# A two-attention, two-convolution kernel: all six instruction orders rewritten, finer pool waits, whole-row statistics for three blocks

## The chip, the cores and the metric

One core of a Trainium2 chip runs the whole program. Its engines work in parallel, each through its own list of instructions in order: TensorE (PE, matmuls into PSUM), VectorE (DVE), ScalarE (ACT), GpSimd (POOL), and SyncE (SP), which here issues nearly all DMAs. The metric is device time in microseconds, and less is better. The profile is one execution, recorded instruction by instruction.

## The reference

The input `x` has 2048 rows of 512 columns (bf16). Four residual layers follow one another, with the same weights for both layers of a kind:

```python
x = x + _A_ref(_layernorm(x), A_wqkv, A_wo)          # attention
x = x + _B_ref(_layernorm(x), B_A_re, ..., B_Dskip)  # convolution
x = x + _A_ref(_layernorm(x), A_wqkv, A_wo)
x = x + _B_ref(_layernorm(x), B_A_re, ..., B_Dskip)
```

`_A_ref` projects to queries, keys and values with 32 heads of 16 columns. Each row attends to 8 rows: itself and those 2, 4, ... 14 rows earlier (earlier than the first row: masked). Softmax over the 8, weighted sum of values, projection by `wo`. `_B_ref` is a long convolution: per column a kernel of 2048 taps is made from 128 complex exponentials, `K[d, l] = Re sum_n C[d,n] exp(dt[d] A[d,n] l) dt[d] B[d,n]`; `K` and the layer's input are transformed by FFT, multiplied and transformed back; the input times `Dskip` is added.

## The kernel before

Row `16 p + a` of `x` lies in partition `p` (0 to 127), slot `a` (0 to 15). A *block* is four slots (512 rows), so there are four blocks.

The order of the work is written out by hand in six strings. A character or token is one step, and each string is walked from left to right; what a step issues goes to the end of the lists of the engines that it uses. So a string sets the order on every engine at once. Engines still run ahead of each other, held by semaphores alone.

**ORDERK** (`k_gen`): the convolution's taps and the front of the first attention. `s`, `i` square the complex exponentials (`s` on ACT, `i` on DVE), `b` copies powers into the tables `B_t` and `pow_t` on ACT, `c` copies a plane of `pow_t` by DMA, `C` and `M` are complex products on DVE, `G` builds Fourier constants on ACT. `T` and `U` build the power table `A_t` on DVE in four column chunks, even chunks in one pair of tiles (`T`), odd ones in another (`U`); `H` opens the next chunk with an ACT copy, and the first `H` opens the second pair of tiles in a pool of its own. `p` are the matmuls that make taps from tables, `x` their evictions into the kernel rows `kgs`, which 24 DMAs store at the end. For the attention: `a` row statistics on ACT (blocks 0 to 2), `3` on DVE (block 3), `l` and `W` norms, `y` and `z` normalised rows, `t`/`e` transposes and evictions, `k`/`K` and `q`/`Q` projections and evictions, `E` and `o` shifted copies of keys, `X` the first three products of queries and keys, `Z` their sums.

**CORE0, CORE1** (`LayerA.core`): the rest of each attention. `m` multiplies queries by keys (DVE, `prod`), `l` sums over head columns (PE), `x`, `e`, `r`, `n`, `T` are the softmax, `v`/`q` projections, `P` multiplies attention by values (DVE, `pav`), `S` or `V` sums it (PE, in half or whole columns), `O` projects by `wo`, adds the residual and takes statistics; `b`, `d` are norm steps, `t` statistics on DVE, `a` and `f` the normalised row on DVE or ACT. In CORE0 `A` to `H` copy eight parts of the convolution kernel, on the engines that `KROWS` lists (D = DVE, A = ACT).

**ORDER0, ORDERF, ORDER1** (`FftB.run`): the convolutions. The last letter of a token is the engine of its eviction (A = ACT, D = DVE, G = POOL and DVE in turn, B = ACT and DVE in turn). `K` and `U` transform kernel and input, `k` and `u` do the second transform step (`u` evicts on ACT into `ub`), `m` multiplies the two spectra on DVE. There are 16 of each, eight per half of the columns. `y` (64-row matmuls) and `Y` (128-row) are the first inverse step, again 16: those of a half need all eight `m` of that half. `z g b` is the last inverse step for half `g` and block `b`; `w g c b` and `v g c b` do it for a quarter of the columns, for eight or four slots. On DVE it adds the residual, on ACT extra matmuls with the identity add it. All these matmuls go through four rotating PSUM buffers. In the first convolution `k` takes a buffer from a list, `m` gives two back and issues a store to `kf_dram`, and loads on SP swap rows; the 16th `K` adds eight buffers. In the second one `m` reads spectra that SP loads from `kf_dram`.

ORDERF ends the first convolution and begins the second attention: `h g b` takes statistics over half rows (four instructions of 256 columns), `H b` over whole rows (four of 512), `a`, `p`, `n` make norms and normalised rows, `T`, `E`, `P`, `Q` transpose, evict and project. A whole-row step needs both halves of its block, a half step one.

A pool that takes over the room of a closed pool waits, as a rule, for everything that used the old one. With `reuse_waits="tile"` a new tile waits only for the tiles whose room it takes.

Of the kernel before, what the change touches and what calls it, by code (L numbers as in the profile page):

```python
# [11 lines left out]
ALU = mybir.AluOpType  # L12
# [34 lines left out]
sCiibsCbiisCiiMbMCGMiMsabiMcbiasMbbCCaGiMMTsibGGTGTicMbGsbiaTbcisbbTTTMGiiTbTiMaGsaGGTMiGacMabTl  # L47
MlMMMWMlaiMsiMayMwMiMybyaTMysteMMqatMaaMkeMadTkqMialKMMlQMkWMlaqMMcbqykTQHqUaUKqQaakUTyqUkyqUUpU
KUkyUapxUxtaUpatpeUaldHQqeUqkKUkl3TT33TQkkxpWl3KxTpTxyxTylTWTpqlkyyTqpHKkzkQzxKUtkUktezUqqeUKTkT
kQKztktkTeeKkUkUKTTkkKUUUkUxUUpxEUpkxpUkUUkpEKkKqxpkUxoxpEoKXqUokUkQUpKxpZxXxZXZ  # L50
"""
ORDER0 = """
KD KA KA KA KD KA KD KA KD KA KD kA kD kA kA kD UA KD UA UD kA UA kD UA KD UA
UD UA KD kA u UD m UA KA u UD u UD m KA u kA m m UA u u kD m m u
UA u UD kA m UA kD kA u m kA kD u kA yA m YD m u m u YA u u m u
yA m m u yA m m YA yA yD yD
# [3 lines left out]
yA yA z01D yA z00D yA yD h00 yA h01 YA v100A v110A v102A v013A h10 a0 p0 n0G z02A v111A v101A S v112A  # L60
h02 h11 T0 E00A a1 E01A z13D p1 n1G v003A P03 Q00 h12 a2 P01 T1 E10A p2 P00 E11D n2G h03 P11 P12
P13 T2 E20A h13 a3 E21D P02 p3 n3D P22 P21 P10 T3 E30D E31D P23 P20 x1
"""
ORDER1 = """
UA UD UA UD UA UA UD UA UD UA UD u UD u u UA m u m u m UA m u m u
UD m m UA u m u m u u yA YA u m m u yD m YA m u u m m u yA
YA m yA YD w000D yA yA yD yA z03D yA w010D yA yD yA z02D v103A v113D v112D v102D v110D v100A v111D v101A
# [3 lines left out]
vvmvvlvmvvmlvxlemvrmnlqmqvlTvqlxevqmlvmvmPvvP1rnllxS0qTmqOeVmrqP4qSl2OPPSOSOPSmPP5On3l8ml6SPCOOV  # L71
AlxSPP7eOSrObSPn9POSdOESOPSPbDadBPfaGOtFOaaawVfHSbatO
"""
CORE1 = """
0m1l2ml3mvvqqlmmlmvqqvvllxmemqvlrnvvlmxTqqlvvmqlmvPvvvvmvqlleqVPrmxqmnqSTOePlPmSOPllSPOSPrOSnOPS
mOSPOblxOSPPdeOSrffbVPdfwOnPfVOPSOSPafbOPSdafftOSafatO
# [4 lines left out]
KROWS = "ADDAADAA"  # L81
# [913 lines left out]
def k_gen(tc, nc, a_consts, ins, kd, la, x_v, lnst, zero, b_consts):  # L995
# [3 lines left out]
    with ExitStack() as ctx:  # L999
# [94 lines left out]

        def power(k):
            if 3 <= k <= 7:
                nc.scalar.copy(Pw[:, :, k - 3, 1::2, :].rearrange("p c r x -> p r c x"), planes(k))
            else:
                nc.scalar.copy(Bt[:, :, :, B_L.index(1 << k), :], cur[k][:].rearrange("p r (q g) -> p r q g", g=4))

        def power_neg(k):
            nc.scalar.mul(Pw[:, :, k - 3, 2, :], planes(k)[:, 1], -1.0)
# [51 lines left out]
        def norms():  # L1154
            D2 = D * D
            for b in range(4):
                cs = slice(4 * b, 4 * b + 4)
                rstd = la.fp.tile([P, 4], F32, name="ln_rstd")
                nb = la.fp.tile([P, 4], F32, name="ln_nb")
                ln[b] = rstd, nb  # L1160
                if b < 3:
                    mean, ms = lnst["s1"][:, cs], -1.0 / D
                    msq = la.fp.tile([P, 4], F32, name="ln_msq")
                    veps = la.fp.tile([P, 4], F32, name="ln_veps")
                    lvar[b] = veps[:]
                    yield lambda: nc.vector.scalar_tensor_tensor(msq[:], mean, -1.0 / D2, mean, ALU.mult, ALU.mult)
                    yield lambda: nc.vector.scalar_tensor_tensor(veps[:], lnst["s2"][:, cs], 1.0 / D, msq[:], ALU.mult, ALU.add)
                else:
                    ag = la.fp.tile([P, 4, 2], F32, name="ln_ag")
                    lvar[b] = ag[:, :, 1]  # L1170

                    def aggr():
                        for a in range(4):
                            nc.vector.bn_aggr(ag[:, a, :], lnst["bn"][:, 12 + a, 0, :])

                    yield aggr
                    mean, ms = ag[:, :, 0], -1.0
                yield lambda: nc.vector.scalar_tensor_tensor(nb[:], mean, ms, rstd[:], ALU.mult, ALU.mult)
# [17 lines left out]
        def turned(b, d):  # L1196
            nc.scalar.copy(la.xnT[:, 2 * d:2 * d + 2, b * 512:(b + 1) * 512], xps[b, d][:].rearrange("p t a q -> p t (a q)"))
# [9 lines left out]
        def projected(kind, b, ft):  # L1207
            dst = la.kT[:, ft, 14 + b * 4:18 + b * 4, :] if kind == "k" else la.qT[b][:, ft]
            nc.scalar.copy(dst.rearrange("p a q -> p (a q)"), pps[kind, b, ft][:])  # L1209
# [3 lines left out]
        def stage_two():  # L1213
            c_small.close()
            tab.append(ctx.enter_context(tc.tile_pool(name="kg_tab1", bufs=1)))
            late["kgp"] = ctx.enter_context(tc.tile_pool(name="kg_out", bufs=1))
# [53 lines left out]
        def produced(c, q8):  # L1270
# [3 lines left out]
            nc.scalar.copy(late["kgs"][:, :, q0:q0 + 8].rearrange("p m (h j) -> p m h j", h=2),  # L1274
# [42 lines left out]
        def chain(*fs):  # L1317
# [3 lines left out]
        fts = range(NDT)  # L1321
# [4 lines left out]
            a=calls(pass_stats, *((b, a, i) for b in range(3) for a in range(4) for i in range(2))), l=norms(),  # L1326
            W=calls(inv_std, *((b,) for b in range(4))), y=calls(apply, *((b, a, "act") for b in range(3) for a in range(4))),
            z=calls(apply, *((3, a, "dve") for a in range(4))),
# [9 lines left out]
        ops["3"] = calls(lambda a: row_stats(nc, lnst, xb[3][:, a, :], 12 + a, "dve"), *((a,) for a in range(4)))  # L1338
# [240 lines left out]
```

## Time and profile before

| | us |
|---|---|
| median of 3 runs | 402.94 (402.64 to 403.21) |
| profiled execution | 402.72 |
| its span, first to last instruction | 400.8 |
| DVE busy | 381.5 (95%) |
| ACT busy | 326.0 (81%) |
| PE busy (matmuls) | 320.0 (80%) |
| POOL busy | 66.1 (17%) |

The granted TensorE clock is 0.999. Busy time is the union of an engine's instructions, which overlap a little: the time from start to start is shorter than the duration of one. A line of the timeline gives the start, the time, engine, source line, operation, result and operands, the number of like instructions merged, and in brackets idle time of that engine just before, with the engine whose work ended it. The largest groups are the DVE products of the attentions (`pav` at L465, 72.6 us in 34, and `prod` at L340, 66.6 us in 29) and the evictions of the convolutions on ACT (`ub` at L865, 31.9 us in 32).

### The profile page before, as it was taken

What the parts mean: (1) busy time and instruction counts of PE and PEld (TensorE: products, weight loads), DVE (VectorE), ACT (ScalarE), POOL (GpSimd) and SP (SyncE); (2) the same over time, 40 slices, a digit from 0 to 9 for tenths busy, and PEclk for the clock granted to TensorE, in tenths of its full rate; (3) what the DMA queues carried; (4) which work ended last, traced back from release to release, by engine and by line L of the source; (5) the groups of instructions that cost most, each with busy time, mean ns of one, the idle gap of its engine ahead of it and who ended that gap; (6) DMA issues with size and microseconds to landing.
All of it is one profiled execution on the core that took longest, in us unless ns stands there. A gap on an engine that the chain in (4) does not pass through costs nothing.

```text
span 400.8 us, 14761 instructions
## 1 busy us (share of the span) xinstructions
PE 320.0 (80%) x6479; PEld 227.6 (57%) x6527; DVE 381.5 (95%) x475; ACT 326.0 (81%) x565; POOL 66.1 (17%) x79
## 2 busy tenths in 40 slices
PE   3000178789999899889997889999999998998795
PEld 2000037557635567656887878643456766667785
DVE  6999999999999999999999999979999999989995
ACT  7999999786656499888999998864655788989983
POOL 9402500000299600030500002300000001000000
PEclk9999999999999999999999999999999999999999
DMA  7942820323014855285235677740063009504606
GB/s 220 395 132 31 87 65 12 83 54 94 12 39 110 216 180 152 79 296 225 101 115 206 223 270 215 263 136 2 2 169 94 3 20 404 162 2 108 213 11 205
DMA packets 62322, 54.17 MB, mean 135 GB/s; under 512 B 33869, under 2 KB 50738, under 8 KB 60978
## 3 DMA queue, kind: packets, MB, share of 16 engines
q1 hardware_dynamic: 62250, 53.22, 43.6%
q8 instruction: 51, 0.84, 0.9%
q14 instruction: 13, 0.11, 0.1%
q10 hardware_dynamic: 8, 0.00, 0.0%
HBM read 30.15 MB, written 13.24 MB: 108 GB/s over the span
## 4 chain that ended last, share of the span: by engine, by line
PE 29%; DVE 21%; issue 9%; ACT 7%; DMA 4%; SPq 1%; POOL 0%; DVEq 0%; ACTq 0%
DVE pav L465 5%; PE pq L396 5%; PE pq L501 4%; PE po L490 4%; DVE prod L340 3%; PE pq L221 3%; DVE t L849 3%; DVE t L852 3%; DVE ln_bn L148 2%; PE pb L799 2%; DMA v_ext<-v_ext 2%; PE L L352 2%; DVE a1s L788 1%; PE pb L806 1%; PE pb L883 1%
## 5 line engine op out<-in xcount | busy, mean ns | idle before, releaser
L465 DVE TENSOR_TENSOR pav<-attn,v_ext 128x4096 bf16<-128x4096 bf16 (+1 forms) x34 | 72.6, 2169 | 0.2
L340 DVE TENSOR_TENSOR prod<-qT,kT_ext 128x4096 bf16<-128x4096 bf16 x29 | 66.6, 2322 | 0.4 <-ACT qT L223 0.3
L1108 DVE TENSOR_TENSOR A_t<-A_t,pow_t 128x1024 bf16<-128x1024 bf16 (+4 forms) x46 | 37.9, 870 | 0.2
L1194 PE MATMUL pt<-ident,x_blk 128*128 128x128 bf16 x64 | 6.3, 241 | 39.6 <-ACT x_blk L193 39.6
L501 PE MATMUL pq<-wop,oT 128*128 128x512 bf16 x122 | 31.7, 379 | 3.4 <-issue 2.5
L490 PEld LDWEIGHTS <-pav 64*128 64x128 bf16 x1664 | 26.0, 95 | 13.4 <-DVE pav L465 6.0
L490 PE MATMUL po<-ident,pav 64*128 64x64 bf16 x1664 | 29.0, 190 | 4.2 <-DVE pav L465 2.3
L865 ACT CAST ub<-pb 128x1024 bf16<-128x1024 f32 x32 | 31.9, 1068 | 0.2
L398 ACT CAST v_ext<-pq 128x512 bf16<-128x512 f32 x32 | 18.8, 586 | 16.1 <-PE pq L396 16.1
L1204 PE MATMUL pp<-xnT,kT_ext 128*128 128x512 bf16 x88 | 25.3, 404 | 7.8 <-ACT qT L1209 2.8
L806 PE MATMUL pb<-a1s,w_sb 128*128 128x64 bf16 x768 | 27.3, 193 | 5.0 <-ACT a1s L788 3.1
L396 PE MATMUL pq<-wv,xnT 128*128 128x512 bf16 x120 | 29.9, 379 | 0.4
L806 PEld LDWEIGHTS <-w_sb 128*128 128x128 bf16 x768 | 24.8, 98 | 7.2 <-issue 4.8
L1194 PEld LDWEIGHTS <-x_blk 128*128 128x128 bf16 x64 | 4.7, 107 | 42.0 <-ACT x_blk L193 40.4
L788 DVE CAST a1s<-pb 128x1024 bf16<-128x1024 f32 x21 | 24.7, 1214 | 2.5 <-PE pb L799 2.2
L788 ACT CAST a1s<-pb 128x1024 bf16<-128x1024 f32 x27 | 26.4, 1043 | 0.8 <-PE pb L799 0.8
L1266 PEld LDWEIGHTS <-A_t 128*64 128x64 bf16 (+1 forms) x512 | 21.9, 103 | 4.7 <-DVE A_t L1108 0.6
L1266 PE MATMUL pk<-B_t,A_t 128*64 128x84 bf16 (+1 forms) x512 | 23.7, 201 | 1.0 <-ACT kgs L1274 0.5
L221 PE MATMUL pq<-xnT,kT_ext 128*128 128x512 bf16 x92 | 23.0, 379 | 0.2
L176 POOL TENSOR_TENSOR ln_rstd<-ln_rstd,ln_mh 128x4 f32<-128x4 f32 x2 | 4.0, 2016 | 107.4 <-DVE ln_rstd L175 107.4
L396 PEld LDWEIGHTS <-xnT 128*128 128x128 bf16 x128 | 11.7, 97 | 14.3 <-issue 1.7
L492 ACT CAST oT<-po 128x512 bf16<-128x512 f32 x26 | 14.9, 575 | 5.8 <-PE po L490 5.8
(261 smaller groups left out, 902.9 us busy)
## 6 DMA issues: line engine op xcount, KB each, us to landing
w_sb<-w_dram SPq DMA_DIRECT2D x8, 1024.0 KB, 6.8
w_dram<-xnT SPq DMA_DIRECT2D x1, 4096.0 KB
kf_ring<-kf_dram SPq DMA_DIRECT2D x13, 256.0 KB, 4.5
kf_ring<-kf_dram SPq DMA_DIRECT2D x26, 128.0 KB, 3.9
v_ext<-v_ext SPq DMA_DIRECT2D x4, 784.0 KB, 6.4
x_blk<-in_A_x_dram SPq DMA_DIRECT2D x4, 512.0 KB, 4.7
kT_ext<-in_A_wqkv_dram SPq DMA_DIRECT2D x4, 512.0 KB, 9.5
x_sb<-in_A_x_dram SPq DMA_DIRECT2D x4, 512.0 KB, 6.1
```

The lines of the kernel that those rows point to most:

```text
L221: nc.tensor.matmul(pq[:], lhsT=self.wqk[:, dt, ft * P:(ft + 1) * P], rhs=self.xnT[:, dt, q * 512:(q + 1) * 512], start=(dt == 0), stop=(dt ...
L340: nc.vector.tensor_tensor(pr, self.qT[q][:, ft].unsqueeze(1).to_broadcast([P, W, 4, P]), kap, ALU.mult)
L396: nc.tensor.matmul(pp[:], lhsT=xnT[:, dt, a * P:(a + 1) * P], rhs=wv[:, dt, :], start=(dt == 0), stop=(dt == NDT - 1))
L465: nc.vector.tensor_tensor(pv[:, i], attn[:, n % 4].unsqueeze(2).to_broadcast([P, W, DH // parts, H]), vap, ALU.mult)
L490: nc.tensor.matmul(po[:, h, 0, i * nt + ft, :], lhsT=pvf[rows, i, w, ft * P:(ft + 1) * P], rhs=ident[rows, rows], start=(w == 0 and ft + i ...
L501: nc.tensor.matmul(pw[:], lhsT=oT[:, ftp, :], rhs=self.wo[:, ftp, :], start=False, stop=(ftp == NDT - 1))
L788: (self.nc.scalar.copy if eng == "act" else self.nc.vector.tensor_copy)(dst, src)
L806: nc.tensor.matmul(p2[:, j, :], lhsT=self.w2[:, ec * EC + j, :], rhs=a1s[:, ec * EC + j, :], start=True, stop=True)
L865: nc.scalar.copy(ub[:], p2)
L1108: return lambda: nc.vector.tensor_tensor(*args)
L1204: nc.tensor.matmul(pps[kind, b, ft][:], lhsT=la.wqk[:, dt, c:c + P], rhs=la.xnT[:, dt, b * 512:(b + 1) * 512], start=(dt == 0), stop=(dt = ...
L1266: nc.tensor.matmul(o, lhsT=lhs, rhs=Bt[:, ri, c * CH + ql].rearrange("p b g -> p (b g)"), start=(not half and j % 4 == 0 and ri == 0), sto ...
```

## The change

All six strings are written anew. The choice of engine for many evictions, until now fixed in the code, is read from a table `ENGK`; as filled in, it differs from before in four places only: one `y` row goes from ACT to DVE, three of the four `z` rows of block 3 from DVE to ACT. `KROWS` gives DVE four parts rather than three. `STATD` names the block with DVE statistics, block 3 as before. The pools of the second power table and of the kernel rows get `reuse_waits="tile"`. In ORDERF three of the four blocks use `H` in place of two `h`. Inside the strings the engines shift too. On DVE are, before and after: in ORDER0 8 and 5 `K`, 6 and 7 `U`, 6 and 8 `k`; in ORDER0 and ORDERF together 4 and 4 `y` or `Y`, 3 and 2 `z`, 0 and 1 `v`; in ORDER1 4 and 5 `y` or `Y`, 4 and 1 `z` or `w`, 5 and 5 `v`; in CORE0 6 and 5 `a`; in CORE1 4 and 6 `a`.

```diff
 ORDERK = """
-sCiibsCbiisCiiMbMCGMiMsabiMcbiasMbbCCaGiMMTsibGGTGTicMbGsbiaTbcisbbTTTMGiiTbTiMaGsaGGTMiGacMabTl
-MlMMMWMlaiMsiMayMwMiMybyaTMysteMMqatMaaMkeMadTkqMialKMMlQMkWMlaqMMcbqykTQHqUaUKqQaakUTyqUkyqUUpU
-KUkyUapxUxtaUpatpeUaldHQqeUqkKUkl3TT33TQkkxpWl3KxTpTxyxTylTWTpqlkyyTqpHKkzkQzxKUtkUktezUqqeUKTkT
-kQKztktkTeeKkUkUKTTkkKUUUkUxUUpxEUpkxpUkUUkpEKkKqxpkUxoxpEoKXqUokUkQUpKxpZxXxZXZ
+siaCCibCsbCCiiaMisbMiGCsMbMiTibMisGiMGbMbsibMcbcisTbTbTiicMGTsbcTbGGiGMTiiaTbTMsaMMaaiaMsGbMMilG
+MaiGaGlTMMiWlayyTcMTMMaTMyytbMwTMMMteaaqaesaMlTadqliaMMWMMQklkMqKqbMykMMHkQqUaKaypUyqUkakUaUyQUU
+UUUUpxKqxtqtaaQUkkpUepKxkeUHqxdTTqlkTaQplkKTTxkTWp3lpyETT3yKq33qxyTQlyqWpqHTQktxkktkKTUUeUeKlUUz
+zTzkkTzUkTKktxkUUkUKUUetkUpUkpKUxpexkKUkUUpKkkkUxpUoUxKkkKxoKpExqqpEQXXpZoxXxZZ
 """
 ORDER0 = """
-KD KA KA KA KD KA KD KA KD KA KD kA kD kA kA kD UA KD UA UD kA UA kD UA KD UA
-UD UA KD kA u UD m UA KA u UD u UD m KA u kA m m UA u u kD m m u
-UA u UD kA m UA kD kA u m kA kD u kA yA m YD m u m u YA u u m u
-yA m m u yA m m YA yA yD yD
+KD KA KA KA KD KA KD KA KD KA KD kA KA kD KA kD kA UD UA UD KA UA UD kA kD UA
+kD KA UD KA UA kD UA kD u UD m kA u UD UA u UA m m UA kD u u kD kA m
+m u UA UD m u kA u u m kA m kA m u u u m m u YD m u YA YA u
+m yA u YA m m m
 """
 ORDERF = """
-yA yA z01D yA z00D yA yD h00 yA h01 YA v100A v110A v102A v013A h10 a0 p0 n0G z02A v111A v101A S v112A
-h02 h11 T0 E00A a1 E01A z13D p1 n1G v003A P03 Q00 h12 a2 P01 T1 E10A p2 P00 E11D n2G h03 P11 P12
-P13 T2 E20A h13 a3 E21D P02 p3 n3D P22 P21 P10 T3 E30D E31D P23 P20 x1
+yA YD YA yA yD yA z00D yA yA yA yD h00 yA v100A v011A v110A h10 a0 v001D p0 z11A z02A n0G z12A
+v103A H1 S T0 a1 E00A E01D p1 n1B z03D P00 P02 T1 H2 E10A a2 P01 p2 E11D Q00 v113A P10 P03 n2G
+H3 P12 P11 T2 a3 E20D p3 n3D E21A P13 P22 x1 P21 T3 E30A E31D P20 P23
 """
 ORDER1 = """
-UA UD UA UD UA UA UD UA UD UA UD u UD u u UA m u m u m UA m u m u
-UD m m UA u m u m u u yA YA u m m u yD m YA m u u m m u yA
-YA m yA YD w000D yA yA yD yA z03D yA w010D yA yD yA z02D v103A v113D v112D v102D v110D v100A v111D v101A
+UA UD UA UD UA UA UD UA UD UA UD UD u m u UA UA u m UD u u m u m UA
+m u m u m m u m u m u u YD m YA u YA yD m yA YA m u u u m
+w001A m w000A m YA yA yD yA YA w011D yA w010A yD yA yD yA v103D v102A v112D v113D v100D v110A v111A v101D
 """
 
 CORE0 = """
-vvmvvlvmvvmlvxlemvrmnlqmqvlTvqlxevqmlvmvmPvvP1rnllxS0qTmqOeVmrqP4qSl2OPPSOSOPSmPP5On3l8ml6SPCOOV
-AlxSPP7eOSrObSPn9POSdOESOPSPbDadBPfaGOtFOaaawVfHSbatO
+mvvqvlmqvlmvlxvevvrqmlmnlmvvxTvelmqvmlvqmvvlv1PrlPnqSqTOmSmqxOePSrPOVP0n2l8SPPOSPm3O54SlOl6AVmP7
+lxPOSPOeSPOr9SwbDnOSPOSdPPCaOSGOfbaPVdfFaOBStfbEtaaHO
 """
 CORE1 = """
-0m1l2ml3mvvqqlmmlmvqqvvllxmemqvlrnvvlmxTqqlvvmqlmvPvvvvmvqlleqVPrmxqmnqSTOePlPmSOPllSPOSPrOSnOPS
-mOSPOblxOSPPdeOSrffbVPdfwOnPfVOPSOSPafbOPSdafftOSafatO
+0m1l2ml3mmqqqlvvvlqmxmvelvrvmvnllqmvqlmvTqxvmlvmPelvvPqmvvvqlqmrlnxSTmOPeSqSOPSPlOrSOPmPnSPlqOSl
+mOSlOPObxSPebdPfVradaOSfPOwVnfPPOSOPSfOPSbOtdaaafatSfO
 """
 ROWS0 = (0, 2, 1, 3, 4, 5, 6, 7, 8, 9, 10, 11, 12, 13, 14, 15)
 ROWS1 = (0, 2, 1, 3, 4, 5, 6, 7, 8, 9, 10, 11, 12, 13, 14, 15)
 NCOL = (2, 2)
-KROWS = "ADDAADAA"
+ENGK = dict(b="AAAAAAAAAAAAAAAAA", y="AAAAAAADAAAA", z="AADA", e="AAAAAAAA", K="AAAAAAAAAAAAAAAA", Q="AAAAAAAA", x="AAAAAAAAAAAAAAAA")
+STATD = (3,)
+KROWS = "ADDADAAD"
...
+        def copy_by(eng):
+            return nc.scalar.copy if eng == "A" else nc.vector.tensor_copy
+
         def power(k):
+            copy = copy_by(ENGK["b"][k + max(0, min(k - 3, 5))])
...
-            z=calls(apply, *((3, a, "dve") for a in range(4))),
+            z=calls(apply, *((3, a, by[ENGK["z"][a]]) for a in range(4))),
...
-            tab.append(ctx.enter_context(tc.tile_pool(name="kg_tab1", bufs=1)))
-            late["kgp"] = ctx.enter_context(tc.tile_pool(name="kg_out", bufs=1))
+            tab.append(ctx.enter_context(tc.tile_pool(name="kg_tab1", bufs=1, reuse_waits="tile")))
+            late["kgp"] = ctx.enter_context(tc.tile_pool(name="kg_out", bufs=1, reuse_waits="tile"))
```

## The prediction

> **What bounds the kernel now.** I read the page's busy shares first, then the busy time of each engine in six stretches that I cut by the six order strings: front (0 to 111 us), first attention (to 191), first convolution (to 237), its end with the front of the second attention (to 269), second attention (to 351), second convolution (to the end).
>
> ```profile
> PE 320.0 (80%) x6479; PEld 227.6 (57%) x6527; DVE 381.5 (95%) x475; ACT 326.0 (81%) x565; POOL 66.1 (17%) x79
> ...
> 0.00:111.00 111.00, 58.24 (x723) 39.05 (x733) 106.33 (x172) 96.67 (x178) 25.05 (x50) 1.00 0.42 107
> 111.00:191.00 80.00, 72.12 (x1480) 46.06 (x1497) 79.35 (x64) 60.60 (x122) 29.42 (x16) 1.00 0.54 165
> 191.00:237.00 46.00, 39.70 (x1216) 36.72 (x1211) 43.55 (x59) 45.34 (x52) 5.27 (x7) 1.00 0.47 168
> 237.00:269.00 32.00, 31.25 (x489) 22.48 (x484) 28.16 (x76) 25.09 (x42) 5.38 (x7) 1.00 0.70 229
> 269.00:351.00 82.00, 78.54 (x1494) 48.35 (x1511) 81.05 (x58) 57.87 (x124) 1.02 (x1) 1.00 0.32 105
> 351.00:400.80 49.80, 40.17 (x1109) 34.98 (x1102) 43.06 (x51) 40.45 (x51) 0.00 (x0) 1.00 0.37 108
> ```
>
> After the stretch and its length the columns are PE, PEld, DVE, ACT and POOL busy. VectorE (DVE) is the bound of the front (its 4.7 us of idle time lie before 9.2 us) and of both attentions (0.65 and 0.95 us idle). In the first convolution ScalarE (ACT) is as full as DVE. From 237 to 269 PE is the fullest, 31.25 of 32. The last stretch has two halves:
>
> ```profile
> 357.00:384.40 27.40, 23.08 (x685) 21.38 (x680) 27.36 (x25) 27.25 (x31) 0.00 (x0) 1.00 0.40 119
> 384.40:400.80 16.40, 11.86 (x369) 10.74 (x366) 11.25 (x13) 8.54 (x11) 0.00 (x0) 0.99 0.44 131
> ```
>
> Until the last multiplication by the spectrum ends (384.4) DVE and ACT are both full. After it PE works 11.86 of the 12.3 us to the last matmul at 396.7; an ACT copy and the last store (3.5 us) follow. DVE in that half:
>
> ```profile
> 378.65 5.75 DVE L849 TENSOR_TENSOR t<-ub,kf_ring 128x2048 bf16<-128x2048 bf16 x5
> 384.33 1.21 DVE L788 CAST xnT<-pb 128x1024 bf16<-128x1024 f32 x1
> 385.46 1.21 DVE L931 TENSOR_TENSOR x_sb<-pb,x_sb 128x1024 bf16<-128x1024 f32 x1
> 386.59 1.21 DVE L788 CAST z<-pb 128x1024 bf16<-128x1024 f32 x1
> 388.39 1.22 DVE L912 TENSOR_TENSOR x_sb<-pb,x_sb 128x1024 bf16<-128x1024 f32 x1 [0.58 <-PE pb L909]
> 389.96 1.23 DVE L931 TENSOR_TENSOR x_sb<-pb,x_sb 128x1024 bf16<-128x1024 f32 x1 [0.35 <-PE pb L929]
> ```
>
> The reader is to see that DVE waits for PE here, not the reverse.
>
> **The steps that I count with** are from start to start. A 1024-element eviction or add out of PSUM: 1.14 on DVE (three in 3.47), 0.91 on ACT. A spectrum multiplication: 1.14 in the last stage (five in 5.75), 1.2 in the first (two of 0.6). A 512-element add on DVE 0.61, eviction on ACT 0.48. A normalised row: 0.33 on DVE (three in 1.07), 0.72 on ACT, 0.55 on DVE beside POOL (two in 1.11). Statistics: 0.34 a half row (twelve in 4.13), 0.61 a whole one. On PE: 0.58 for a `y`, 0.95 for a `Y`; 0.86 and 1.3 for a `z` or `w` without and with the matmuls that add the residual (its ACT form needs them, the DVE form not), 0.45 and 0.67 for a `v`. The sum goes against the profiled run, 402.72 us (span 400.8 and 1.9 around it), 0.22 below the median 402.94.
>
> **The change part by part.**
>
> *Front.* One `y` row goes to DVE, three `z` rows leave it: DVE -2 x 0.33 = -0.66, ACT +2 x 0.72 = +1.4. The ACT gaps of 60 to 109 us (1.11, 0.61, 1.62, 1.06 among them) cover that; without them it costs up to 1.4. The rest of ORDERK is the same work. I followed squarings, powers and products by hand to the second table: no DVE wait appears. Pools: the one idle time before the table's first copy (ACT, L1225) is 0.2 us, so the finer wait gains 0.2 at most; its new place right behind the last `M`, with no DVE work between it and the first `U`, would cost 0.6 if it still waited. I take 0. The third table's copy (second `H`) had 5.2 us of DVE work between it and the `T` that reads it (two `U` of 2.2, statistics) and now has none; behind the copy on ACT stand norms and table products. 0 to +1.1, the longest ACT wait for such a product; I take 0.2, as ACT comes up there about when DVE does. The last three `X` follow all `U`, so the 24 `kd` stores on SP (16 us from 108.08) start some 2 us earlier; `v_ext` DMAs queued behind them gain slack, not time. Front: -0.5.
>
> *First attention.* One apply leaves DVE (-0.33), KROWS gives it one more kernel row block (+0.33). DVE idle can only grow from 0.65. The 16th `v` comes one or two PE projections (0.87 each) later; its `v_ext` DMA landed 142.1, the product needing it began 144.8, so about 1 us of slack stays. Bounds -0.6 to +1; I take 0.2.
>
> *First convolution.* `K` 8 DVE/8 ACT becomes 5/11, `U` 6/10 becomes 7/9, `k` 6/10 becomes 8/8. Up to the last `m` DVE keeps 21 casts and 16 products (43.1 us); ACT loses two `y`, which now follow that `m`. Fewer ACT evictions could fill DVE's 2.2 us of gaps: -2.2. Against that, `k12` to `k15` take buffers freed 2.4 to 3.5 us of DVE work earlier (5.8 to 8.2 before), while a `kf_dram` store lands 3.5 to 3.9 after issue; behind a waiting `k` on ACT stand the `ub` evictions for which `m` waits: 0 to +3. SP issues the same loads and stores, unblocked by `m` for longer, since the 16th `K` opens the ring eleven tokens sooner. Followed eviction by eviction with four PSUM buffers, the last `m` ends 0.2 earlier. I take 0.
>
> *End of it and second front.* DVE: a 1024 add less (-1.14), a 512 add more (+0.61), three blocks of whole rows -3 x (8 x 0.34 - 4 x 0.61) = -0.8, block 1's two DVE rows without POOL -0.4: -1.8 together. POOL loses 1.69 of work, ACT gains two rows (1.5). But PE and the chain to the first `prod` set the end. Three `y` of the first half now stand between the last `m` and the second half's `y` on ACT. Following the chain from the last `m`: first norm at 10.9 us (before 11.6), block 1 at 15.5 (16.9), block 2 at 21.0 (20.8), block 3 at 25.7 (26.0), first `prod` at 32.7 (32.5). DVE's -1.8 becomes more idle time. Bounds -1.8 and +1.4 (four PE `y` of 0.58 minus what runs in the shadow); I take +0.2.
>
> [...] DVE is at 28.16 of 32 there. [...]
>
> *Second attention.* Two more applies on DVE, +0.66, with DVE full; the row statistics `b` for rows 8 to 11 move behind the last `pav`, where DVE then has 3.8 us before the last row's statistics against PE's 3.05. I take +0.7 in all; ACT's -1.4 is worth nothing.
>
> *Second convolution.* DVE: `z`/`w` adds go from four to one (-3.4), one more `y` (+1.14), -2.3 together. The `y` lies before the last `m`, where DVE is full: that `m` ends 1.14 later. The relief lies after it, where PE binds. PE's work behind the last `m`: before 8 x 0.58 + 2 x 0.86 + 0.9 (`w`) + `v` 5 x 0.45 + 3 x 0.67 = 11.5; after 7 x 0.58 + 0.95 + 0.9 + 1.3 + 4.3 = 11.5. The two `w` on ACT, put ahead of it, use PE's idle time. Of 0.6 us of PE gaps (two of them waits for DVE, 0.35) some 0.35 go. So +1.14 - 0.35 = +0.8. Bounds: -2.3 if DVE bound the tail, +2 if PE's extra 2 us (three identity sets of 0.44, two `Y` for `y`) all show.
>
> **Sum:** -0.5 + 0.2 + 0 + 0.2 + 0.7 + 0.8 = +1.4 on 402.72, so 404.1; 404.0 rounded down, since half of it rests on +0.7 and +0.8 that the first convolution's gaps may partly pay.
>
> **The rivals.**
>
> *DVE's savings arrive (faster).* Place: DVE in the last two stages named. Summed over the kernel it does -0.66 - 0.5 - 0.8 - 0.4 + 0.66 - 2.3 = -4.0. If DVE sets the time there as it does at 95% over the span, 402.9 - 4.0 = 398.9; from a fifth of it on (0.8) the change is measurably faster. For it: the busy share. Against it: the waits for PE in the fence above. [...] Chance 0.30, time 398.9 to 401.8.
>
> *Nothing measurable.* The terms of +0.7 and +0.8 meet the 2.2 us that the first convolution can give back: 403. Chance 0.24.
>
> *A new wait in the front or first convolution (slower still).* The third table's copy (+1.1), `k12` to `k15` behind their stores (+3), or the twelve first-half statistics that now wait for their second halves and so lose their place in DVE's gaps (12 x 0.34 = +4.1): one of them on top of 404.0 gives 405.5 to 408. For it: each has lost its cover in the new order. Against: DMA slots open sooner. Chance 0.14.
>
> **How the numbers follow.** My forecast (403.8 to 405.3) has 0.32. Faster by over 0.2% (below 402.1; 0.2% is about what a measurement of this kernel tells from no change) is the first rival with 0.30 and a little of the second: 0.32. Within it 0.22, slower 0.46. The range takes in the first rival's middle and the new waits up to +3: 400.0 to 407.0.
>
> **What would show it.** Right: from the last `m` of the second convolution to the last matmul again about 12 us, DVE idle above 3 us in it, and that `m` about 1.1 us later after the stage's first cast; DVE busy near 378; the first `prod` of the second attention 32 to 34 us behind the first convolution's last `m`. Wrong: that tail shorter than 11 us, a DVE wait above 1 us before a `T` or `k`, or the first convolution from first cast to last `m` (47.85 us now) more than 1.5 us off.

## The result, and the profile after

The changed kernel takes 405.69 us (median; 402.76 to 407.31), the kernel before beside it on the same chips 403.25 us (402.54 to 404.56). The ratio is 1.0049, interval 1.0034 to 1.0064: slower by half a per cent. The forecast was 404.0, range 400 to 407. Measured again beside the experiments the same kernel had 1.0066 (1.0040 to 1.0093). Its 20 executions scatter over 4.5 us, the 20 of the kernel before over 2 us (85 later ones of the kernel before, beside the experiments, over 4.6: 401.8 to 406.4). A good part of the loss turns out to sit in that scatter, so a single profile shows only some of it. The profiled execution took 404.53 us, span 402.8 (before: 402.72 and 400.8).

The busy shares of the page of the changed kernel:

```profile
PE 329.1 (82%) x6507; PEld 228.9 (57%) x6507; DVE 376.4 (93%) x461; ACT 328.8 (82%) x568; POOL 55.6 (14%) x77
```

DVE does 5.1 us less than before, and the span is 2.0 longer. So DVE's sum was not what bound the kernel. The same six stretches, cut at the changed kernel's own marks, and the two halves of the last one; the columns are those of the prediction (stretch, length, busy PE, PEld, DVE, ACT, POOL, clock, DMA share, GB/s):

```profile
0.00:110.00 110.00, 59.41 (x717) 39.10 (x718) 105.38 (x170) 97.08 (x178) 17.25 (x49) 1.00 0.42 108
110.00:190.00 80.00, 75.56 (x1532) 46.83 (x1531) 78.01 (x62) 61.70 (x124) 27.56 (x15) 1.00 0.55 170
190.00:235.00 45.00, 40.36 (x1128) 36.40 (x1122) 43.93 (x62) 44.74 (x51) 6.06 (x8) 1.00 0.53 190
235.00:269.00 34.00, 32.00 (x484) 22.91 (x485) 26.99 (x66) 27.12 (x45) 3.70 (x5) 1.00 0.49 154
269.00:351.00 82.00, 79.72 (x1544) 46.85 (x1542) 80.78 (x58) 55.56 (x121) 1.02 (x1) 1.00 0.36 116
351.00:402.80 51.80, 42.01 (x1120) 36.76 (x1112) 41.34 (x50) 42.58 (x53) 0.00 (x0) 0.99 0.36 105
...
357.20:385.70 28.50, 25.07 (x703) 23.16 (x697) 28.46 (x25) 28.11 (x32) 0.00 (x0) 1.00 0.39 114
385.70:402.80 17.10, 11.38 (x356) 10.85 (x356) 8.06 (x10) 9.48 (x12) 0.00 (x0) 0.97 0.43 126
```

The stretch of the second front (from the last `m` to the first product) is now cut at 34.0 us where it was 32 (33.9 and 32.4 by the marks below), and DVE has 7 us of idle time in it. In the second convolution DVE and ACT are full up to the last `m`, which ends at 385.8, as before; behind it DVE works 8.06 us instead of 11.25, and PE 11.38 against 11.86. DVE behind the last `m`, from its timeline:

```profile
386.52 1.23 DVE L790 CAST z<-pb 128x1024 bf16<-128x1024 f32 x1 [0.74 <-PE pb L885]
388.87 1.23 DVE L933 TENSOR_TENSOR x_sb<-pb,x_sb 128x1024 bf16<-128x1024 f32 x1 [1.13 <-PE pb L931]
391.47 2.36 DVE L790 CAST z<-pb 128x1024 bf16<-128x1024 f32 x2 [1.37 <-PE pb L885]
...
397.25 0.69 DVE L933 TENSOR_TENSOR x_sb<-pb,x_sb 128x512 bf16<-128x512 f32 x1 [0.79 <-PE pb L931]
```

With 0.15 us before another add these waits are 4.2 us: DVE waits for PE longer than before, and the work taken from it there has become idle time.

All profiled executions, cut at marks of the DVE and ACT timelines: first product of the first attention, first cast of the first convolution, end of its last `m`, first product of the second attention, first cast of the second convolution, end of its last `m`, end of the last computation, end of the span. The columns are the lengths between them, in us. The experiments e1 to e12 are told below.

| profile | front | 1st attention | 1st convolution | 2nd front | 2nd attention | 2nd convolution | tail | last stores | span |
|---|---|---|---|---|---|---|---|---|---|
| before | 109.60 | 79.17 | 47.93 | 32.42 | 87.40 | 27.88 | 12.88 | 3.52 | 400.8 |
| changed | 108.71 | 80.12 | 46.19 | 33.86 | 87.87 | 29.03 | 12.16 | 4.86 | 402.8 |
| e1 changed, again | 109.71 | 79.51 | 46.31 | 34.11 | 87.89 | 29.02 | 12.17 | 3.88 | 402.6 |
| e2 | 108.77 | 80.79 | 47.16 | 34.81 | 87.95 | 27.89 | 12.86 | 4.37 | 404.6 |
| e3 | 108.76 | 79.41 | 46.26 | 32.84 | 87.89 | 29.02 | 12.59 | 3.83 | 400.6 |
| e4 | 110.15 | 79.71 | 50.46 | 33.85 | 87.87 | 29.03 | 12.17 | 4.66 | 407.9 |
| e5 | 108.55 | 79.28 | 46.76 | 33.17 | 88.93 | 29.02 | 12.71 | 3.48 | 401.9 |
| e6 | 108.49 | 80.94 | 46.03 | 32.72 | 88.36 | 29.01 | 12.85 | 4.10 | 402.5 |
| e7 | 108.79 | 79.40 | 46.74 | 34.48 | 87.90 | 29.03 | 12.17 | 3.89 | 402.4 |
| e8 | 108.81 | 79.81 | 46.54 | 32.95 | 87.56 | 27.89 | 12.86 | 4.08 | 400.5 |
| e9 | 108.78 | 80.41 | 46.01 | 33.33 | 88.99 | 29.01 | 12.17 | 4.40 | 403.1 |
| e10 | 108.79 | 81.52 | 46.02 | 33.82 | 87.86 | 29.02 | 12.17 | 5.30 | 404.5 |
| e11 | 108.77 | 79.61 | 46.85 | 34.33 | 87.87 | 29.02 | 12.17 | 5.58 | 404.2 |
| e12 | 108.83 | 79.37 | 46.42 | 32.78 | 87.56 | 27.89 | 12.87 | 3.68 | 399.4 |

Some columns repeat to 0.1 us and follow the order string alone (second convolution and most of the second attention). Others move by 1 to 4 us between executions of the same instructions: the first convolution under the new ORDER0, the second front under the new ORDERF, the last stores under any order.

### The profile page after: what moved, and what is told of

Its sections match the earlier page's. It is cut to its first block, busy times and chain, and to the rows that moved or that the text cites. A ratio compares the mean times of both kernels' runs of the same rounds, so it can differ in the third digit from the quotient of the medians.

```text
span 402.8 us, 14751 instructions
## 1 busy us (share of the span) xinstructions
PE 329.1 (82%) x6507; PEld 228.9 (57%) x6507; DVE 376.4 (93%) x461; ACT 328.8 (82%) x568; POOL 55.6 (14%) x77
## 5 line engine op out<-in xcount | busy, mean ns | idle before, releaser
L492 PEld LDWEIGHTS <-pav 64*128 64x128 bf16 x1728 | 27.0, 95 | 15.5 <-DVE pav L467 9.1
L492 PE MATMUL po<-ident,pav 64*128 64x64 bf16 x1728 | 30.3, 190 | 4.8 <-DVE pav L467 2.8
L1213 PE MATMUL pp<-xnT,kT_ext 128*128 128x512 bf16 x96 | 28.3, 426 | 5.8 <-ACT xnT L1206 2.9
L503 PE MATMUL pq<-wop,oT 128*128 128x512 bf16 x128 | 32.9, 379 | 0.0
L398 PE MATMUL pq<-wv,xnT 128*128 128x512 bf16 x128 | 31.4, 379 | 0.3 <-ACT kgs L1283 0.3
L790 ACT CAST a1s<-pb 128x1024 bf16<-128x1024 f32 x29 | 27.9, 1031 | 1.4 <-PE pb L801 1.2
L225 ACT CAST qT<-pq 128x512 bf16<-128x512 f32 x24 | 14.1, 587 | 13.1 <-PE pq L223 13.0
L790 DVE CAST a1s<-pb 128x1024 bf16<-128x1024 f32 x19 | 22.6, 1216 | 1.8 <-PE pb L801 1.7
L223 PE MATMUL pq<-xnT,kT_ext 128*128 128x512 bf16 x96 | 24.2, 380 | 0.0
L509 ACT ACTIVATE x_sb<-pq 128x512 bf16<-128x512 f32 x24 | 14.3, 595 | 8.1 <-PE pq L503 8.0
L398 PEld LDWEIGHTS <-xnT 128*128 128x128 bf16 x128 | 11.5, 97 | 14.7 <-issue 2.8
```

Source lines behind the costliest of these rows:

```text
L223: nc.tensor.matmul(pq[:], lhsT=self.wqk[:, dt, ft * P:(ft + 1) * P], rhs=self.xnT[:, dt, q * 512:(q + 1) * 512], start=(dt == 0), stop=(dt ...
L398: nc.tensor.matmul(pp[:], lhsT=xnT[:, dt, a * P:(a + 1) * P], rhs=wv[:, dt, :], start=(dt == 0), stop=(dt == NDT - 1))
L492: nc.tensor.matmul(po[:, h, 0, i * nt + ft, :], lhsT=pvf[rows, i, w, ft * P:(ft + 1) * P], rhs=ident[rows, rows], start=(w == 0 and ft + i ...
L503: nc.tensor.matmul(pw[:], lhsT=oT[:, ftp, :], rhs=self.wo[:, ftp, :], start=False, stop=(ftp == NDT - 1))
L790: (self.nc.scalar.copy if eng == "act" else self.nc.vector.tensor_copy)(dst, src)
L1213: nc.tensor.matmul(pps[kind, b, ft][:], lhsT=la.wqk[:, dt, c:c + P], rhs=la.xnT[:, dt, b * 512:(b + 1) * 512], start=(dt == 0), stop=(dt = ...
```

## The experiments

Times are medians beside the kernel before; the ratio is against it, with its interval.

### Which order string carries the loss (e1 to e4)

e1 is the changed kernel itself.

> The changed kernel unchanged, as the measure for the three kernels beside it, and with a second profile. Its times so far spread from 402.8 to 407.3 us, those of the kernel before from 402.5 to 404.6. Theory E (the end): the spread and part of the loss lie behind the last computation, where the first profile has 4.9 us (397.94 to 402.8) against 3.5 before; then a profile with a span above 404 has more than 4.9 us there and the stages ahead of it stand within 0.5 us of the first profile's. Theory S (the stages): a longer span shows as longer DVE waits in the stages, the stretch behind the last computation stays between 3.5 and 5 us. Time expected by both: 403 to 407 us, ratio 1.003 to 1.007.

Measured: 406.12 us (402.78 to 408.8), 1.0066 (1.0040 to 1.0093). Both theories hold a part. The last stores take 3.5 to 5.6 us over all profiles, under the old ORDER1 (3.52, 4.37, 4.08, 3.68) and the new alike, so they scatter, and are not what the change did. The longer spans of e2 (404.6) and e4 (407.9) show in the stages, as theory S has it.

e2 takes the old ORDER1 back:

```diff
 ORDER1 = """
-UA UD UA UD UA UA UD UA UD UA UD UD u m u UA UA u m UD u u m u m UA
+UA UD UA UD UA UA UD UA UD UA UD u UD u u UA m u m u m UA m u m u
...
```

> Changed kernel with the old ORDER1 (the order of the second convolution), all else as changed. By the prediction's sum that stage costs +0.8 (its last product of the spectrum 1.14 us later, less 0.35 of gaps): the time comes down by 0.8 us, and the last m ends 1.1 us earlier after the stage's first cast. Theory E: the 1.4 us behind the last computation belong to the new order of the stores too, so the time comes down by 1.5 to 2.4 us, to the kernel before or below it, and the stretch behind the last computation is 3.5 us again. If DVE's 2.3 us less of work in this stage had been worth anything, the time would go up instead, by 0.2 to 2.3.

Measured: 406.10 us, 1.0066 (1.0041 to 1.0091): no change against e1. In the stages the last `m` does come 1.13 us earlier (29.02 to 27.89) and the tail grows by 0.69, so the stage is worth 0.44, not 0.8; that is too little to see beside an interval of 1 us each way. Theory E, which had 1.5 to 2.4, falls.

e3 takes ORDER0 and ORDERF back:

```diff
 ORDER0 = """
-KD KA KA KA KD KA KD KA KD KA KD kA KA kD KA kD kA UD UA UD KA UA UD kA kD UA
+KD KA KA KA KD KA KD KA KD KA KD kA kD kA kA kD UA KD UA UD kA UA kD UA KD UA
...
 ORDERF = """
-yA YD YA yA yD yA z00D yA YA yA yD h00 yA v100A v011A v110A h10 a0 v001D p0 z11A z02A n0G z12A
+yA yA z01D yA z00D yA yD h00 yA h01 YA v100A v110A v102A v013A h10 a0 p0 n0G z02A v111A v101A S v112A
...
```

> Changed kernel with the old ORDER0 and ORDERF (first convolution, its end, the second front), all else as changed. The traces say: from the first cast to the last m 1.74 us longer again (46.1 back to 47.85), from there to the second attention's first product 1.44 shorter (33.9 back to 32.5), together +0.3. The prediction's terms for the two are 0 and +0.2: the time comes down by 0.2 us at most. [...]

Measured: 403.42 us, 1.0002 (0.9980 to 1.0024). That is 2.7 us below e1 on the same chip, where at most 0.2 was expected, and takes the whole loss back. Its first convolution takes 46.26 us without the new ORDER0, so the 1.7 us that the traces of before and after seemed to give to that order are not its own. All twelve profiles with the new start have 46.0 to 47.2 there. Whether the start brings that, or the one profile of the kernel before was long there by chance (one cast on DVE waits 0.8 us for a store of the spectrum, one on ACT 0.5), is not shown; in the whole the new start alone gains no measurable time (e8). The second front is back at 32.84. A fall of this size would also fit a cost of the whole rows; e7 tests that by itself.

e4 keeps the new orders from ORDER0 on and takes the start back (ORDERK with its engines, CORE0, KROWS):

```diff
-ENGK = dict(b="AAAAAAAAAAAAAAAAA", y="AAAAAAADAAAA", z="AADA", e="AAAAAAAA", K="AAAAAAAAAAAAAAAA", Q="AAAAAAAA", x="AAAAAAAAAAAAAAAA")
+ENGK = dict(b="AAAAAAAAAAAAAAAAA", y="AAAAAAAAAAAA", z="DDDD", e="AAAAAAAA", K="AAAAAAAAAAAAAAAA", Q="AAAAAAAA", x="AAAAAAAAAAAAAAAA")
...
-KROWS = "ADDADAAD"
+KROWS = "ADDAADAA"
```

> Changed kernel with the old ORDERK, its old engines for the twelve y and four z rows, and the old CORE0 with KROWS: front and first attention as before, all else as changed, with the pools' finer waits kept. The prediction's terms for these are -0.5 and +0.2: the time rises by 0.3 us. The two traces have -0.9 and +0.95: no change (within 0.2 us).

Measured: 407.64 us, 1.0113 (1.0084 to 1.0143), 1.5 us above e1, more than either expectation, though the two intervals overlap. Its profile is the most disturbed one, with a first convolution of 50.46 us. The waits there from 224 to 231 us (engine, line, what it waited for, us, times, longest):

```profile
DVE t L854 <- ACT ub L867: 2.7, 1, 2.7
PE pb L808 <- ACT kn L790: 1.4, 1, 1.4
PE pb L808 <- ACT kf_sb L790: 1.3, 1, 1.3
ACT kn L790 <- DMA kf_dram<-kn: 1.1, 1, 1.1
ACT kf_sb L790 <- DMA kf_dram<-kf_sb: 0.9, 1, 0.9
```

Read from below: two casts of `k` on ACT wait for a store of the spectrum, PE waits for these casts, and behind them on ACT stand the `ub` for which DVE waits. And the same microseconds in stretches of one:

```profile
226.00:227.00 1.00, 0.23 (x8) 0.23 (x8) 0.91 (x2) 0.72 (x1) 0.00 (x0) 1.00 0.89 326
227.00:228.00 1.00, 0.40 (x14) 0.31 (x11) 0.00 (x0) 0.33 (x1) 0.00 (x0) 0.80 0.71 258
228.00:229.00 1.00, 0.27 (x6) 0.27 (x6) 0.00 (x0) 1.00 (x2) 0.00 (x0) 0.50 0.86 313
229.00:230.00 1.00, 1.00 (x18) 0.98 (x16) 0.37 (x1) 1.00 (x2) 0.00 (x0) 0.50 0.80 266
...
234.00:235.00 1.00, 1.00 (x17) 1.00 (x16) 1.00 (x3) 0.83 (x1) 0.00 (x0) 0.78 1.02 373
```

After two microseconds with PE 23 to 40% busy the granted clock (the third number from the end) is 0.50 for some seven us; from 229 on PE is busy all the time in them, with 13 to 18 matmuls in a microsecond, where 222 to 224 have 29 and 33. In e2 the same casts wait 0.18 and 0.52 us, the clock is 0.50 from about 226.4 to 229.8, and the stage takes 47.16. In the two profiles of the changed kernel they do not wait; in the first DVE waits 0.69 for `ub`, and the clock there stays at 1.00. So some tenths of a wait more go with 1 us (e2) and 4 us (e4) more in the stage, and half clock is a part of that.

### Which half, and the whole rows (e5 to e8)

e5 has the old ORDER0 before the new ORDERF, e6 the new ORDER0 before the old ORDERF, each with the `y` fitted so that all 16 are done once:

```diff
 ORDERF = """
-yA YD YA yA yD yA z00D yA YA yA yD h00 yA v100A v011A v110A h10 a0 v001D p0 z11A z02A n0G z12A
+yD yA z00D yA YA yA yD h00 yA v100A v011A v110A h10 a0 v001D p0 z11A z02A n0G z12A
...
```

```diff
 ORDERF = """
-yA YD YA yA yD yA z00D yA YA yA yD h00 yA v100A v011A v110A h10 a0 v001D p0 z11A z02A n0G z12A
+YA yA yD yD yA yA z01D yA z00D yA yD h00 yA h01 YA v100A v110A v102A v013A h10 a0 p0 n0G z02A v111A v101A S v112A
...
```

> Changed kernel with the old ORDER0 up to and behind the last m, and the new ORDERF without the four y that the old ORDER0 has done already. Splits the 2.6 us that the old ORDER0 and ORDERF together gave back (406.1 to 403.4). Theory K (the casts of the last k wait for the stores of the spectrum, which stand in SP's queue behind the exchange loads of later blocks): the loss is in the first convolution, the time is 403.4 to 404. Theory P (in the second front PE stops for 0.7 to 1.7 us in the middle of a y, waiting for nothing that the profile shows, and the first norm comes later): the loss stays, 405 to 406. If the whole rows of statistics cost the time, it stays as well.

> The other half: changed kernel with the new ORDER0, then the last four y of the old ORDER0 and the old ORDERF. Theory K: the loss stays, 405.5 to 406. Theory P, or the whole rows: 403.4 to 404.5. If both halves carry it, both kernels come out near 404.7.

Measured: e5 403.70 us, 1.0033 (1.0011 to 1.0055); e6 405.08 us, 1.0041 (1.0019 to 1.0063). By the ratios each half carries some of it: they are 0.3% and 0.4% above that of e3, and e1 is 0.6% above it. Each interval overlaps that of e3 a little, so neither half is sure by itself. The median of e5 is where theory K puts it, but five of its eleven executions took 404.8 to 408.3 us. The second front is 33.17 and 32.72 against 33.86 and 34.11 with both new strings, and neither profile has the stop of PE that the next fences show.

In the second front of the changed kernel DVE and PE stop, each from its own timeline:

```profile
241.38 1.23 DVE L790 CAST z<-pb 128x1024 bf16<-128x1024 f32 x1 [2.29 <-PE pb L885]
```

```profile
239.72 0.19 PE L885 MATMUL pb<-WpJ,t 64*128 64x64 bf16 x1
240.62 0.20 PE L885 MATMUL pb<-WpJ,t 64*128 64x64 bf16 x1 [0.71 <-issue]
```

PE stops between two matmuls of one `y`, waiting for nothing that the profile shows. With the new ORDER0 and ORDERF together (in e7 and e11 with their edits) it does so in every profile but one, in the same `y`: 0.71, 0.96 (e1), 1.68 (e2), 0.73 (e4), 0.69 (e7), 0.67 (e10), 1.18 (e11). The exception is e9, below.

e7 takes row blocks 1 to 3 in half rows again, inside the new order:

```diff
-v001D p0 z11A z02A n0G z12A
-v103A H1 S T0
+v001D p0 h01 z11A z02A n0G h02 z12A
+v103A h11 S T0
...
-T1 H2 E10A
+T1 h12 E10A
...
-H3 P12 P11 T2
+h03 h13 P12 P11 T2
```

> Changed kernel with row blocks 1 to 3 taken in half rows again (eight statistics of 256 elements for four of 512, the first half of each ahead of its place in the old manner), all other tokens in the new order. DVE does 3 x (8 x 0.34 - 4 x 0.61) = 0.8 us more. [...]

Measured: 408.31 us, 1.0129 (1.0106 to 1.0152), 2.2 us above e1: half rows cost time at these places, and more than the 0.8 us of work that they add. In the stage its profile has 34.48 us against 33.86 and 34.11. Five of its six executions have a mean granted clock of 0.987 to 0.992, so half clock may have a part in the rest; where it fell in them is not seen, for the profiled execution is the shortest of the six (405.65).

e8 has the new start and nothing else of the change but the finer waits of the pools:

```diff
 CORE1 = """
-0m1l2ml3mmqqqlvvvlqmxmvelvrvmvnllqmvqlmvTqxvmlvmPelvvPqmvvvqlqmrlnxSTmOPeSqSOPSPlOrSOPmPnSPlqOSl
+0m1l2ml3mvvqqlmmlmvqqvvllxmemqvlrnvvlmxTqqlvvmqlmvPvvvvmvqlleqVPrmxqmnqSTOePlPmSOPllSPOSPrOSnOPS
...
```

(ORDER0, ORDERF and ORDER1 as in e2 and e3.)

> The new ORDERK with its engines, the new CORE0 and KROWS and the finer waits of the pools, and everything behind them (ORDER0, ORDERF, CORE1, ORDER1) as before. By the stage times of the two traces the front gives 0.85, the first attention takes 0.2 to 0.9: 402.4 to 403.3 against some 403.4 before. Beside the kernel with the old ORDER0 and ORDERF (403.4) it also has the old CORE1 and ORDER1, for which the traces have 0.5 and 0.4: so 402.5. By the prediction's terms (-0.3, and 0.7 and 0.8): 403.1 against before and 1.5 below that kernel.

Measured: 402.84 us, 0.9991 (0.9975 to 1.0006). The new start is worth 0.8 us at the first product and no measurable time in the whole. Against e3 (1.0002) the old CORE1 and ORDER1 give 0.0011, some 0.4 us, which the intervals do not tell from nothing; the stages have 0.33 for the one (87.89 to 87.56) and 0.44 for the other (41.19, second convolution and tail in most profiles, to 40.75); the prediction had 1.5 for the two.

### The stores of the spectrum (e9 to e12)

In the first convolution each `m` sends its block of the spectrum to HBM, and SP issues these stores in one queue with the loads that exchange the rows of later blocks. SP's timeline in the changed kernel:

```profile
207.99 2.86 SPq L836 DMA_DIRECT2D kf_nat<-kf_sb  x4
210.88 0.58 SPq L857 DMA_DIRECT2D kf_dram<-kn  x1
211.57 2.38 SPq L836 DMA_DIRECT2D kf_nat<-kf_nat  x4
214.00 1.64 SPq L857 DMA_DIRECT2D kf_dram<-kn  x1
```

SP issues like this from 204.9 to 233 us with no gap longer than 0.2 (not from 196, as it is put for e9 below: from 202.7 to 204.9 it issues nothing). Before, it starts again only at 208.9:

```profile
203.70 0.58 SPq L855 DMA_DIRECT2D kf_dram<-w_sb  x1
208.92 1.11 SPq L834 DMA_DIRECT2D w_sb<-kn  x2
```

The 16th `K` comes earlier in the new ORDER0, opens eight more tiles, and so puts exchange loads ahead of stores. e9 lets POOL issue the stores:

```diff
-            self.nc.sync.dma_start(self.kf_dram[g, ec].rearrange("p r q e -> (p r) (q e)"), kn.rearrange("p q e -> p (q e)"))
+            self.nc.gpsimd.dma_start(self.kf_dram[g, ec].rearrange("p r q e -> (p r) (q e)"), kn.rearrange("p q e -> p (q e)"))
```

> Changed kernel; the sixteen stores of the spectrum to HBM in the first convolution are issued by POOL instead of SP, where they stand behind the exchange loads (in the trace SP issues without a break from 196 to 233 us). Theory K: the casts of the last k wait for these stores, PE's gaps between 218 and 228 us come from that, and in some executions half clock follows (0.5 from 226.3 to 229.5 and from 227.6 to 234.4 us in the two longest profiles). Then no cast of a k waits for a store, no half clock near 226, and the time falls from 406 to 404 or 405 (what is left is the second front's). Theory D: it is the transfers themselves that are late, not their place in the queue: then the waits and the time stay. A store from POOL may land later; then the waits grow and the time rises.

Measured: 404.65 us (402.98 to 405.48), 1.0025 (1.0010 to 1.0040) against 1.0049 and 1.0066: 1.0 to 1.7 us off the changed kernel and inside the 404 to 405 of theory K, though the interval still touches both of the others. The first convolution takes 46.01 us with no wait of a cast for a store and full clock. POOL's timeline shows when the stores go now:

```profile
221.22 0.54 POOL L857 DMA_DIRECT2D kf_dram<-kn  x1 [3.12 <-ACT kn L790]
223.98 0.54 POOL L857 DMA_DIRECT2D kf_dram<-kn  x1 [2.21 <-ACT kn L790]
224.89 0.54 POOL L857 DMA_DIRECT2D kf_dram<-kf_sb  x1 [0.38 <-ACT kf_sb L790]
```

A store needs only the cast, not the product, and in these lines POOL issues it right behind the cast. The last leaves at 224.9, on SP at 231.7; DMA is idle from 228 to 234 (share 0.06, before the edit 0.96), the weights of the second attention are loaded 2.7 us earlier, and the stop of PE in the second front is gone (33.33 us). The cast for which DVE waited 2.29 us then waits

```profile
240.66 1.23 DVE L790 CAST z<-pb 128x1024 bf16<-128x1024 f32 x1 [1.40 <-PE pb L885]
```

How much of the gain comes from the casts of the first convolution and how much from the earlier weights is not shown: in neither profile of the changed kernel does a cast wait for a store, so the profiles do not have the waits that the edit would take away.

e10 keeps the stores on SP and limits the exchange loads:

```diff
-        return self.tag == 0 and len(self.free) > NG * NEC - self.nk
+        return False
```

> Changed kernel; the exchange loads of the first convolution run at most four blocks ahead of the products, where they now also run ahead as soon as tiles are free. The stores then stand in SP's queue behind fewer loads. Theory K: stores leave earlier, the waits of the k casts go, 404 to 405; if four blocks ahead is too few, a DVE product waits for an exchange and the time rises. Theory D: no change, 405.5 to 406.3.

Measured: 405.20 us, 1.0043 (1.0023 to 1.0063). In its profile the casts no longer wait and the stage takes 46.02 us, as theory K has it, but the stop of PE stays (0.67), and half clock falls elsewhere (161.2 to 164.7 us, first attention 81.52). In the median it is between e9 and the changed kernel, its interval overlaps both: it settles nothing by its time.

e11 moves the last three `k`:

```diff
-m u UA UD m u kA u u m kA m kA m u u u m m u YD m u YA YA u
+m u UA UD m u u u m kA m kA m kA u u u m m u YD m u YA YA u
```

> Changed kernel; in ORDER0 the last three k (13, 14, 15) each come one m later, as in the old order, nothing else moved. The wait of the casts for their stores (0.2 to 1.1 us in the disturbed profiles) has one product of 1.2 us more of cover. Theories K and D alike: the waits go, 404 to 405, and the half clock near 226 us with them. If the time stays at 406, the loss of the new ORDER0 is not in these casts.

Measured: 406.91 us, 1.0083 (1.0059 to 1.0108): slower, not 404 to 405. The casts no longer wait for stores, but with two `u` drawn ahead of a `k` another wait took the place (a PE gap of 1.40 us at 218.1 for a DVE cast, DVE 1.4 for `ub`; 46.85 us). The edit was not the clean one it was meant to be, and speaks neither for K nor against it.

e12 is e8 with the one line of e9.

> The kernel of the new start alone (402.84, 0.9991 of before) with the stores of the spectrum issued by POOL. Theory K: the old ORDER0 has such waits too (0.5 to 0.8 us before one cast on DVE and one on ACT in its traces), only one at a time and better covered; they go, the first convolution takes 46.0 to 46.4 us, and the kernel is 0.3 to 0.8 us faster than with the new start alone: 402.0 to 402.5, ratio 0.997 to 0.9985, which would beat both kernels. If the queue only matters where the new order has shortened the cover, it stays at 402.8, ratio 0.999.

Measured: 401.35 us (400.72 to 402.22), 0.9941 (0.9924 to 0.9957). It beats both kernels, by 0.6% and some 1.1%, and its six executions scatter over 1.5 us only. The gain over e8 is more than the 0.8 us that theory K allowed. The wait of a cast for a store that e8's profile has is gone; in e8 it reads

```profile
ACT w_sb L790 <- DMA kf_dram<-w_sb: 0.7, 1, 0.7
```

Its profile is 1.1 us shorter than e8's, but 0.44 of that are in the first attention and 0.40 in the last stores, which the edit does not touch; the first convolution and the second front have 0.12 and 0.17. So it is measured that the store queue is worth some 0.5% here; in which waits, these profiles do not show.

## Why the prediction was right or wrong

The direction was right. As a ratio the loss would put the forecast's base of 402.94 at 404.9, inside the likeliest case (403.8 to 405.3); the median itself, 405.69, lies above it. That the sum came this near is in part luck: by the profile the first convolution is 1.7 us below its term, and the second front and the last stores are 1.2 and 1.3 above theirs.

**Front, -0.5:** -0.9 in the profile, -0.8 to -1.1 in all with the new start but e1 (+0.1), whose front has 6.83 us of half clock. No DVE wait stands behind the third table's copy, so its 0.2 was nothing. Right in sign, undersized.

**First attention, +0.2:** +0.95 in the profile, +0.1 to +1.8 over the other undisturbed ones with the new start. New are DVE waits of 0.81 for the logits and 0.40 for the convolution's first cast. At the middle of them (79.6) it is +0.4, inside the stated bounds.

**First convolution, 0:** this is the step that failed. The profile says -1.74, beyond the 1.5 that I had set as the mark of being wrong, and e3 shows that the order need have no part in that gain. In the median the new ORDER0 costs time (e6 against e3: 0.4%, 1.6 us, with intervals that overlap a little). A mechanism for it was on record as a bound and a rival: the last `k` behind their stores, 0 to +3. It is seen in e2 (casts wait 0.18 and 0.52 us for their stores) and e4 (0.9 and 1.1), and moving the stores to POOL gives 0.2 to 0.4% back (e9). I gave it 0, although the landing of 3.5 to 3.9 us was longer than the cover of 2.4 to 3.5 that I had counted, and reckoned neither with SP's queue, which I had seen to be "unblocked by m for longer", nor with the clock, for which the profile of before, at 1.00 up to the last `m`, gave no cause.

**End of it and second front, +0.2:** +1.44 in the profile, with the first product 33.9 us behind the last `m` (32.7 forecast, 32 to 34 allowed). It is a term mis-sized by 1.2. Some 0.5 of that is the stop of PE in the `y`: without it the same order takes 33.33 (e9). The rest is the chain itself. In e9 the four norms come 11.2, 16.5, 21.7 and 26.6 us behind the last `m`, where the chain had 10.9, 15.5, 21.0 and 25.7: from the first norm to the second it allowed 4.6 us, and they take 5.3, as they did before. Following PE by the lengths of its rows cannot show the stop. DVE's -1.8 did become idle time, as said.

**Second attention, +0.7:** +0.47 (87.87 against 87.40, within 0.1 in eight profiles; in e5, e6 and e9 0.5 to 1.1 more; in e5 and e9 a `pav` product waits 0.6 and 1.0 us for a `v_ext` DMA). **Second convolution, +0.8:** +0.43. The last `m` comes 1.15 later, as forecast; the tail is 12.2 us, DVE idle 4.2 in it, as forecast; only it shrinks by 0.7 where 0.35 was allowed. PE is the fullest engine there: its matmuls are busy for 11.38 us and its weight loads for 10.85 of the 11.5 us from 385.7 to the end of the last matmul at 397.2, DVE for 8.06 and ACT for 9.48 up to the end of the span.

**The end.** The last stores took 1.34 us more in this profile. No term had them, and by the other profiles they are scatter.

**The rivals.** DVE's savings did not arrive (DVE -5.1, span +2.0). The case "a new wait" (405.5 to 408) has the median at its lower edge: of the 20 executions 11 lie in it, 5 in the likeliest case and 4 below that. Whole rows are not what cost the time: the way back to half rows costs more (e7).

## What to carry to other kernels

A wait that is covered by a few tenths in one profile is sure to be covered only in that execution: under the same ORDER0 the casts of `k` wait for no store in the two profiles of the changed kernel, 0.18 and 0.52 us in e2, and 0.9 and 1.1 in e4. Where a store frees a tile, ask which queue it stands in and what was put ahead of it, and try a queue of its own if one is idle. One line for that took 0.5% off here (e8 to e12), as much as all the reordered strings together had added. And judge an order by many executions: the profile of the changed kernel showed its first convolution as a gain of 1.7 us, while the experiments point to its order as a part of the loss.

## What the runs showed of the hardware

**Half clock, in some executions only.** Equal gaps of PE were followed by a granted clock of 0.50 in one execution and not in another. In the front PE has gaps of 2.02 us at 50.6 and 2.89 at 55.3 both in the changed kernel and in e1; here are the stretches that follow, of the one and the other:

```profile
58.00:60.00 2.00, 1.80 (x5) 0.70 (x5) 2.00 (x6) 1.80 (x4) 0.00 (x0) 1.00 0.00 0
60.00:62.00 2.00, 2.00 (x7) 0.62 (x5) 2.00 (x4) 2.00 (x6) 0.00 (x0) 1.00 0.00 0
```

```profile
58.00:60.00 2.00, 1.81 (x8) 0.73 (x7) 2.00 (x6) 1.80 (x4) 0.00 (x0) 0.85 0.00 0
60.00:62.00 2.00, 1.21 (x4) 0.26 (x2) 2.00 (x4) 2.00 (x6) 0.00 (x0) 0.50 0.00 0
```

The stretches at 0.50 ahead of the tail last 3.41 us (e2, e4, e7, e9, e10) or 6.83 (e1, e4). In the 3.41 us ahead of such a stretch PE was busy for 43% (e4), 50% (e2) and 35% (e1), and for the same 35% in the changed kernel (56.00 to 59.41 us), where the clock stayed at 1.00. So the share of PE's busy time ahead does not tell these cases apart; what does is not shown.

Half clock went with lost time in one front and not in others: with 6.83 us of it near 59 us the front of e1 is 1 us longer than that of the changed kernel (109.71 against 108.71), and with 3.41 us those of e2, e7, e9 and e10 are 108.77 to 108.79. Over all executions the mean granted clock is below 0.993 in 29 of 80 with the new ORDER0 and its stores on SP, in 8 of 120 with the old ORDER0, and in 2 of 18 with the stores on POOL (e9, e12). Seven more (one of the 80, six of the 120) have 0.935 to 0.943 and take 402.4 to 404.0 us; they are not counted in, for they are not long. The scatter does not come from this alone: of the 80, the 29 have a median of 406.5 us and the 50 others still 405.6, against 403.4 with the old ORDER0.

**A stop of PE behind a late packet, probably.** The page of the changed kernel counts 51 DMA packets in a queue that it names instruction:

```profile
q8 instruction: 51, 0.84, 0.9%
```

In its trace each of them has 16,384 bytes. PE ran 13,014 instructions (matmuls and weight loads), 255 to a packet, and the packets follow PE's count: from the 12th (158.7 us) to the last (396.1), PE has begun 252 to 263 instructions for each packet up to the start of that one. In all seven profiles with the stop, PE goes on 2.4 to 3.0 us after such a packet starts (238.2 and 240.62 in the changed kernel, 240.8 and 243.29 in e2), and it stops at one place of its list: behind 7,107 recorded instructions in the changed kernel, e1, e2 and e7. In e9, with the same ORDERF, DMA is free earlier (share 0.06 from 228 to 234 us, where the changed kernel has 0.96), that packet starts at 236.8, and PE does not stop. So the stop may be such a packet that comes late, behind 1 MB of weights (two loads of 512 KB, issued at 234.96 and 235.40 in the changed kernel). That is my estimate from these times: it was not tried by itself, and what the packets carry is not shown.
